# Normalizing after the weighted sum instead of inside the transpose, in the first batch of a fused attention, FFN and MoE kernel

## Chip, cores and metric

One Trainium2 chip, one core. The metric is device time in microseconds for one launch of the whole program (attention for two batches, a SiLU feed-forward layer, a top-1 mixture of eight experts). The median of 3 runs of the kernel before is 621.5 us (619.34 to 621.65). PE is the matmul engine (PEld its weight loads), DVE, ACT and POOL are the three elementwise engines, SP issues most DMAs.

## What is computed

The part of the reference that the change touches is the attention of batch 0 (tiles 0 to 5 of 128 queries; 8 heads of 64):

```python
scores = scale * q @ k.T + bias        # scale = 1/8; local band of 96 keys, 8 global keys
scores = where(keep, scores, -1e9)
scores = scores - max(scores)
a = exp(scores)
a = a / (sum(a) + 1e-09)
x = a @ v                              # then transposed to [heads*64, queries] for the FFN
```

The result x of all 12 tiles (two batches of 6) is what the FFN (x @ w_in, SiLU, @ w_out) reads, and its output goes to the experts.

## The kernel before

The work of the attention is cut into slots: slot s handles tile n = s // 4 and the head pair hp = s % 4. The first batch has SB = 24 slots, written by `slot_b` (L870); the second batch has other code (`slot`, L902) and is not changed. Within the first batch a head pair passes through a software pipeline, and one call of `slot_b(s)` issues a step of several pairs, each engine working its instructions off in the order of issue:

- `emit_qk` (L145): for pair s+1, PE multiplies k and q (64 contraction rows, up to 256 columns) for each of two heads into PSUM tiles `qkp`.
- `emit_tb` (L152): for pair s, DVE adds the bias table and takes the row maximum (L160), one instruction for each head; `emit_mx` (L161) turns the two maxima into the bias of the exponential, -max/8 + ln 1024 (L163).
- `emit_exp` (L164): for pair s-1, ACT computes the exponential of each head and its sum `ss` (L170).
- `emit_dg` (L182): for pair s-1, DVE makes the inverse sums (L185, L186), and POOL multiplies the identity matrix by them, giving a diagonal matrix `dg` for each head (L188).
- `emit_tr` (L189): for pair s-3 (LT = 3), PE multiplies the weights t by `dg` (L194). That transposes and normalizes at once. An f32 product of this kind shows up as two MATMUL instructions. A tile has one chunk of keys (the first tile of the batch) or two (the five others), so a slot has 4 or 8 instructions on L194.
- `emit_cp` (L197): copy from PSUM to SBUF, by ACT from slot 8 on (L199), before that by DVE (L198).
- `emit_px` (L200): for pair s-4, PE multiplies v (64 columns of weights) by the transposed weights (L209), 4 or 8 instructions; the sums of a tile land transposed, ready for the FFN, in a PSUM bank `px` (of tag `pv` for odd tiles, `s1` for even ones).
- `emit_xx` (L212), once a tile: `put_xt` (L243) splits `px` into a high part (ACT, L247) and a low part (DVE, L248), both as fp32r, in the FFN's tile `xT`. For tiles 0 to 3 the low part is put off to the next slot (`xlow`).

The PSUM tiles `qkp` and `tp` come from `abank` (L113), which hands out five banks in turn, three in a slot. From slot 8 on every slot also has one step of decoding the FFN's weights on DVE (`dec_op`, L285; L274 to L276), and at set slots weights are split by ACT and POOL (`spl_w`, L291; L296, L297, L301, L303) and loaded by SP. POOL also copies the eight global keys and values (L139, L142).

After slot 23 the FFN of the first four tiles (chunk 0) begins: each step has 24 products of 128x256 (`s1_mm`, L319; two PSUM banks in turn, tags `s1` and `s1b`), tanh and gating on ACT and DVE, and 12 products of 128x512 (L339 to L341), while DVE decodes and POOL splits the next weights. Slots 24 to 27, which finish the pipeline of the first batch, are worked in between the first two steps.

The lines that hold the order of a slot:

```python
if s+1<SB:
    for j in range(2): emit_qk(*divmod(s+1,4),j)
if o3: cp[0]=emit_tr(n3,h3)
if o1: emit_exp(n1,h1)
...
if cur: emit_tb(n,hp,1); emit_mx(n,hp)
if o3: emit_cp(*cp[0],A if DQ<=s<23 else V)
if o1: emit_dg(n1,h1)
if o4: emit_px(n4,h4)
```

Of the kernel before, what the change touches and what calls it, by code (L numbers as in the profile page):

```python
# [10 lines left out]
F32 = mybir.dt.float32  # L11
# [12 lines left out]
def kernel(ctx, tc, qk, v, n_global, n_local, w_in, w_out, wg, w1, w2, out):  # L24
    nc=tc.nc
    B,NT=v.shape[0],v.shape[1]
    H=8; D=64; KC=4; FB=16; NTT=B*NT; LAG=2; LASTF=2; HB=6; PAIR=256; PX=4
# [3 lines left out]
    SB=24  # L31
    LT=3
# [10 lines left out]
    attn=es_a.enter_context(tc.tile_pool(name="attn",bufs=1,side="right"))  # L43
# [12 lines left out]
    ident=const.tile([P,P],F32,name="ident")  # L56
# [4 lines left out]
    def own_first(n): return n%3==1  # L61
# [10 lines left out]
    V=nc.vector; A=nc.scalar; G=nc.gpsimd; T=nc.tensor; S=nc.sync  # L72
# [62 lines left out]
    def glob_k(n,hp):  # L135

        if n%NT in (0,NT-1): return
        k=ring[hp//2][:,hp%2]
        (G if 4*n<SB else V).tensor_copy(k[:,ksl(n),0,0:32],k[:,ksl(n-1),0,0:32])  # L139
    def glob_v(n):  # L140
        if n%NT in (0,NT-1): return
        if 4*n<SB: G.tensor_copy(vpr4[0:32,n%3,0:512],vpr4[0:32,(n-1)%3,0:512])  # L142
        else: V.tensor_copy(vpr[0:32,n%3],vpr[0:32,(n-1)%3])
    qp={}
    def emit_qk(n,hp,j):  # L145
        i=n%NT
        if (n,hp,j) in qp: return
        q=qp[n,hp,j]=abank([P,2,P],"qkp")
        sl=slice(0,2) if i else slice(0,1)
        w=ring[hp//2][j*D:(j+1)*D,hp%2]; z=ksl(n)  # L150
        T.matmul(q[:,sl],w[:,z,1],w[:,z:z+1,0] if i==0 else w[:,0:3:2,0] if z==0 else w[:,z-1:z+1,0],start=True,stop=True)  # L151
    def emit_tb(n,hp,j):  # L152
        i=n%NT; h=2*hp+j; q=qp.pop((n,hp,j))
        if j==0: tt[n,hp]=attn.tile([P,2,2,P],F32,tag="t",name="t",bufs=3) if 4*n>=SB else mp.tile([P,2,2,P],F32,tag="g",name="t",bufs=6)
        t=tt[n,hp]
        if h==0:
            mx[n]=attn.tile([P,H],F32,tag="mx",name="mx",bufs=2); ss[n]=attn.tile([P,H],F32,tag="ss",name="ss",bufs=2)
        sl=slice(0,2) if i else slice(0,1)
        tb=tabs[:,3:4,h,:] if i==0 else (tabs[:,1::-1,h,:] if i==1 else tabs[:,1:3,h,:]) if own_first(n) else tabs[:,0:2,h,:] if i==1 else tabs[:,2:0:-1,h,:]
        V.tensor_tensor_reduce(out=t[:,j,sl],in0=q[:,sl],in1=tb,scale=1.0,scalar=-3e38,op0=ALU.add,op1=ALU.max,accum_out=mx[n][:,h:h+1])  # L160
    def emit_mx(n,hp):  # L161
        h=2*hp+1
        V.tensor_scalar(out=mx[n][:,h-1:h+1],in0=mx[n][:,h-1:h+1],scalar1=-0.125,scalar2=float(np.log(1024.0)),op0=ALU.mult,op1=ALU.add)  # L163
    def emit_exp(n,hp):  # L164
        i=n%NT
        t=tt[n,hp]
        ce=1 if i==0 else 2
        for j in range(2):
            h=2*hp+j
            A.activation(out=t[:,j,:ce],in_=t[:,j,:ce],func=AF.Exp,scale=0.125,bias=mx[n][:,h:h+1],accum_out=ss[n][:,h:h+1])  # L170
    def emit_h(n,hp):
        t=tt[n,hp]; nch=ce=1 if n%NT==0 else 2
        x=attn.tile([P,2,2,nch,P],F16,tag="hl",name="hl",bufs=2); hl[n,hp]=x
        V.tensor_copy(x[:,:,0],t[:,:,:ce])
    def emit_l(n,hp):
# [2 lines left out]
        y=attn.tile([P,2,2,nch,P],F16,tag="pT",name="pT",bufs=3)  # L178
        pT[n,hp]=y
        S.dma_start_transpose(out=y.rearrange("p a b c d -> p (a b c) d"),in_=x.rearrange("p a b c d -> p (a b c d)"))  # L180
    dg={}
    def emit_dg(n,hp):  # L182

        s=ss[n][:,2*hp:2*hp+2]
        V.tensor_scalar(out=s,in0=s,scalar1=1024.0e-9,scalar2=None,op0=ALU.add)  # L185
        V.reciprocal(out=s,in_=s)  # L186
        d=attn.tile([P,2,P],F32,tag="t",name="dg",bufs=3); dg[n,hp]=d
        for j in range(2): G.tensor_scalar(out=d[:,j],in0=ident,scalar1=s[:,j:j+1],scalar2=None,op0=ALU.mult)  # L188
    def emit_tr(n,hp):  # L189

        t=tt.pop((n,hp)); d=dg.pop((n,hp)); ce=1 if n%NT==0 else 2
        m=abank([P,2,ce,P],"tp")
        for j in range(2):
            for c in range(ce): T.matmul(m[:,j,c],t[:,j,c],d[:,j],start=True,stop=True)  # L194
        y=attn.tile([P,2,ce,P],F32,tag="pT",name="pT4",bufs=3); pT[n,hp]=y
        return y,m
    def emit_cp(y,m,e):  # L197
        if e is V: V.tensor_copy(y,m)  # L198
        else: A.activation(out=y,in_=m,func=AF.Copy)  # L199
    def emit_px(n,hp):  # L200

        i=n%NT; ce=1 if i==0 else 2
        if hp==0: pvt[n]=ps.tile([P,KC,P],F32,tag="pv" if n%2 else "s1",name="px",bufs=1)
        y=pT.pop((n,hp))
        vb=[n%3] if ce==1 else [n%3,(n-1)%3] if own_first(n) else [(n-1)%3,n%3]
        for c in range(ce):
            for j in range(2):
                h=2*hp+j
                T.matmul(pvt[n][j*D:(j+1)*D,hp,:],vpr4[:,vb[c],h*D:(h+1)*D],y[:,j,c,:],start=(c==0),stop=(c==ce-1))  # L209
        if hp==3: glob_v(n)  # L210
    xlow=[]
    def emit_xx(n):  # L212
        put_xt(n,pvt[n],xlow if 4*(n+2)<SB else None)
    def emit_pv(n,hp):
        i=n%NT; ce=1 if i==0 else 2
        if hp==0: pvt[n]=ps.tile([P,H,D],F32,tag="pv",name="pv",bufs=1)
        y=pT.pop((n,hp))
        vb=[n%3] if ce==1 else [n%3,(n-1)%3] if own_first(n) else [(n-1)%3,n%3]
        for j in range(2):
            h=2*hp+j  # L220
            for c in range(ce):
                seq=[(0,0),(0,1),(0,2),(1,0),(1,1)]
                for k,(a,m) in enumerate(seq):
                    T.matmul(pvt[n][:,h,:],y[:,j,a,c,:],vpr[:,vb[c],m,h*D:(h+1)*D],start=(c==0 and k==0),stop=(c==ce-1 and k==4))  # L224
    rs={}
# [11 lines left out]
    def emit_xt(n):  # L237
# [2 lines left out]
        for k in range(KC):  # L240
            T.transpose(m[:,k,:],xa[:,2*k:2*k+2,:].rearrange("p a d -> p (a d)"),ident)
        put_xt(n,m)
    def put_xt(n,m,later=None):  # L243
        c,u=divmod(n,2)
        if u==0: xT[c]=mp.tile([P,2,KC,256],F32R,tag="xT",name="xT",bufs=3)
        sl=xT[c][:,:,:,u*P:(u+1)*P]
        A.activation(out=sl[:,0],in_=m,func=AF.Copy)  # L247
        def low(): V.tensor_tensor(out=sl[:,1],in0=m,in1=sl[:,0],op=ALU.subtract)  # L248
        if later is None: low()
        else: later.append(low)  # L250


    wraw={}; wol={}
# [357 lines left out]
    h1={}; hh={}; yp={}  # L611
# [258 lines left out]
    def slot_b(s):  # L870

        ev=[]
        n,hp=divmod(s,4); n1,h1=divmod(s-1,4); n3,h3=divmod(s-LT,4); n4,h4=divmod(s-LT-1,4)
        cur=s<SB; o1=0<=s-1<SB; o3=0<=s-LT<SB; o4=0<=s-LT-1<SB
        def a_():
            if s<SB-3: want(min(s+WL,SB-1))
            elif cur: want(s+3)
            if s==0:
                for j in range(2): emit_qk(n,hp,j)
            if cur: emit_tb(n,hp,0)  # L880
# [3 lines that stand above are left out]
            if o1: emit_exp(n1,h1)  # L884
        ev.append(a_)
        def a2():
            if cur: emit_tb(n,hp,1); emit_mx(n,hp)
            if o3: emit_cp(*cp[0],A if DQ<=s<23 else V)
            if o1: emit_dg(n1,h1)
            if o4: emit_px(n4,h4)  # L890
            if xlow: xlow.pop()()
        ev.append(a2)
        def b_():
            if cur: glob_k(n,hp)
            if h4==3 and o4: emit_xx(n4)
# [44 lines left out]
    with tc.manual_schedule():  # L940
# [7 lines left out]
        s=0  # L948
# [99 lines left out]
```

## Time and profile before

| | us |
|---|---|
| median of 3 runs | 621.5 |
| the profiled execution's own time | 621.69 |
| its span, first to last instruction | 620.0 |
| PE busy in the span | 590.6 (95%) |
| DVE busy | 389.1 (63%) |
| ACT busy | 303.0 (49%) |
| POOL busy | 186.2 (30%) |
| first batch's slots, from 16.62 to the first FFN product | 55.6 |

Times in rows are us from the start of the span. A matmul's recorded duration contains its way through the array, and the next one starts before it ends; so what a stream of matmuls costs is read from start to start, not from the durations. "PE busy" is for the same reason not a measure of how well PE is used.

### The profile page before, as it was taken

Reading aid. Unit: us, or ns where it says so; the run is one execution under the profiler, and the core shown is the slowest. Engines: PE = TensorE matmul, PEld = TensorE weight load, DVE = VectorE, ACT = ScalarE, POOL = GpSimd, SP = SyncE. Lnnn points to the kernel's source line nnn. Section 1 sums busy time; section 2 is a strip of 40 time slices with the busy share of each in tenths; the row PEclk is TensorE's granted clock in tenths of the full one; section 3 lists DMA queues with packets and bytes.
Section 4 is the critical chain, followed back from the end, with each engine's and each line's share of the span. In section 5 each row is a group of like instructions: output and inputs, shape, how many; then the busy total and the mean of one; then the engine's idle time right before and its main releaser. Section 6 shows DMA issues by size and latency. Waiting matters only on the chain.

```text
span 620.0 us, 12009 instructions
## 1 busy us (share of the span) xinstructions
PE 590.6 (95%) x4054; PEld 500.6 (81%) x4054; DVE 389.1 (63%) x1069; ACT 303.0 (49%) x802; POOL 186.2 (30%) x233
## 2 busy tenths in 40 slices
PE   2999899999999999999999999999899999999996
PEld 1566788888888888888889999888788888888884
DVE  4388669999737764756463345744844678778840
ACT  5377634334353445343532234644653666776641
POOL 3367614444314252131221001112231432331321
PEclk9999999999999999999999999999999999999999
DMA  7639725674355587465444327607845378569500
GB/s 255 243 79 355 218 89 159 215 221 158 116 160 148 149 192 170 106 177 130 115 89 141 86 84 259 254 19 246 263 162 185 127 259 269 184 212 290 162 17 21
DMA packets 81511, 105.18 MB, mean 170 GB/s; under 512 B 29978, under 2 KB 44314, under 8 KB 81441
## 3 DMA queue, kind: packets, MB, share of 16 engines
q1 hardware_dynamic: 75712, 94.79, 50.4%
q0 software_dynamic: 2288, 6.39, 2.8%
q10 hardware_dynamic: 3440, 3.15, 1.6%
q8 instruction: 34, 0.56, 0.4%
q14 instruction: 37, 0.30, 0.2%
HBM read 81.46 MB, written 17.99 MB: 160 GB/s over the span
## 4 chain that ended last, share of the span: by engine, by line
PE 69%; issue 8%; DVE 8%; DMA 6%; ACT 4%; POOL 3%; SPq 1%; ACTq 0%; POOLq 0%; DVEq 0%
PE s L319 17%; PE s L339 6%; PE s L340 5%; PE s L341 5%; PE h L616 5%; PE h L622 4%; PE qkp L151 4%; PE y L639 4%; PE y L641 4%; PE y L640 4%; PE tp L194 3%; PE h L617 2%; POOL wol L303 2%; PE pv L224 2%; PE gl L382 1%
## 5 line engine op out<-in xcount | busy, mean ns | idle before, releaser
L319 PEld LDWEIGHTS s<-xT,wi 128*128 128x128 f32 x1152 | 147.3, 190 | 13.1 <-DVE g L328 6.0
L319 PE MATMUL s<-xT,wi 128*128 128x256 f32 x1152 | 152.2, 284 | 1.9 <-DVE xT L248 1.4
L323 ACT ACTIVATE u<-s 128x256 f32<-128x256 f32 x96 | 35.3, 381 | 112.3 <-PE s L319 111.5
L324 DVE SCALAR_TENSOR_TENSOR s<-u,s 128x256 f32<-128x256 f32 x96 | 39.8, 427 | 79.4 <-ACT u L323 79.4
L339 PE MATMUL s<-woh,g 128*128 128x512 f32 x192 | 79.2, 413 | 0.0
L491 DVE TENSOR_TENSOR uq<-qr,uq 128x512 fp32r<-128x512 f32 x87 | 71.2, 841 | 7.2 <-ACT uq L490 4.4
L340 PE MATMUL s<-woh,g 128*128 128x512 f32 x192 | 75.5, 393 | 0.0
L490 ACT ACTIVATE uq<-qr 128x512 fp32r<-128x512 f32 x112 | 66.4, 626 | 4.4 <-DMA qr<-in_w_dram 4.1
L328 DVE TENSOR_TENSOR g<-s,g 128x256 fp32r<-128x256 f32 x96 | 39.3, 422 | 31.7 <-ACT g L327 27.3
L327 ACT ACTIVATE g<-s 128x256 fp32r<-128x256 f32 x96 | 35.7, 380 | 40.3 <-DVE s L324 40.3
L639 PE MATMUL y<-uq,hh 128*128 128x512 f32 (+6 forms) x136 | 55.2, 406 | 0.0
L641 PE MATMUL y<-uq,hh 128*128 128x512 f32 (+6 forms) x136 | 53.6, 394 | 0.0
L640 PE MATMUL y<-uq,hh 128*128 128x512 f32 (+6 forms) x136 | 53.4, 393 | 0.0
L491 POOL TENSOR_TENSOR uq<-qr,uq 128x512 fp32r<-128x512 f32 x25 | 32.9, 1326 | 62.1 <-ACT uq L490 62.1
L151 PE MATMUL qkp<-ring 64*128 64x256 f32 (+1 forms) x192 | 36.0, 455 | 14.3 <-DMA ring<-in_qk_dram 13.4
L170 ACT ACTIVATE t<-t,mx 128x256 f32<-128x256 f32 (+1 forms) x96 | 45.8, 480 | 6.5 <-DVE mx L163 4.6
L631 ACT ACTIVATE hh<-h 128x224 fp32r<-128x224 f32 (+6 forms) x64 | 23.3, 364 | 47.3 <-DVE h L629 27.3
L632 DVE SCALAR_TENSOR_TENSOR hh<-h,hh 128x224 fp32r<-128x224 f32 (+6 forms) x64 | 25.3, 395 | 31.8 <-ACT hh L631 31.8
L339 PEld LDWEIGHTS s<-woh,g 128*128 128x128 f32 x192 | 36.3, 189 | 7.1 <-ACT u L323 2.0
L340 PEld LDWEIGHTS s<-woh,g 128*128 128x128 f32 x192 | 36.3, 189 | 5.0
L577 POOL DMA_INDIRECT out_dram<-y,ixt x17 | 17.4, 1024 | 74.9 <-ACT y L646 56.7
L341 PE MATMUL s<-wolr,g 128*128 128x512 f32 x128 | 39.6, 390 | 0.0
(215 smaller groups left out, 1071.7 us busy)
## 6 DMA issues: line engine op xcount, KB each, us to landing
qr<-in_w_dram SPq DMA_DIRECT2D x128, 256.0 KB
wolr<-wlo_d SPq DMA_DIRECT2D x64, 256.0 KB
wiraw<-in_w_in_dram SPq DMA_DIRECT2D x16, 512.0 KB
wraw<-in_w_out_dram SPq DMA_DIRECT2D x13, 512.0 KB
xe<-zr SPq DMA_DIRECT2D x8, 792.0 KB
wlo_d<-wol SPq DMA_DIRECT2D x16, 256.0 KB
xw<-xe SPq DMA_DIRECT2D x15, 264.0 KB
ring<-in_qk_dram SPq DMA_DIRECT2D x12, 256.0 KB
```

What stands on the lines that cost most here:

```text
L151: T.matmul(q[:,sl],w[:,z,1],w[:,z:z+1,0] if i==0 else w[:,0:3:2,0] if z==0 else w[:,z-1:z+1,0],start=True,stop=True)
L170: A.activation(out=t[:,j,:ce],in_=t[:,j,:ce],func=AF.Exp,scale=0.125,bias=mx[n][:,h:h+1],accum_out=ss[n][:,h:h+1])
L319: T.matmul(t,w[:,ww,kc,:],x[:,xx,kc,:],start=(k==0),stop=(k==11)); k+=1
L324: V.scalar_tensor_tensor(out=t,in0=u,scalar=1.0,in1=t,op0=ALU.add,op1=ALU.mult)
L339: T.matmul(o,g[u][:,0,sl],wh,start=(f==0),stop=False)
L340: T.matmul(o,g[u][:,1,sl],wh,start=False,stop=False)
L341: else: T.matmul(o,g[u][:,0,sl],wl,start=False,stop=(f==FB-1))
L490: A.activation(out=t[:,0],in_=r,func=AF.Copy)
L491: (G if (i%2 if pool is None else pool) else V).tensor_tensor(out=t[:,1],in0=r,in1=t[:,0],op=ALU.subtract)
L639: T.matmul(o,g[:,0,sl],w[:,0],start=(f==0),stop=False)
L640: T.matmul(o,g[:,1,sl],w[:,0],start=False,stop=False)
L641: T.matmul(o,g[:,0,sl],w[:,1],start=False,stop=(f==7))
```

## The change

The exponentials are transposed as they are, by PE's transpose (one instruction for a 128x128 block instead of two), and the division by the sums moves behind the product with v. For that, once a tile, the inverse sums are made for all 8 heads by two DVE instructions, spread by POOL to 512 columns (`rx`), transposed by four PE transposes (`emit_rb`, a fourth PSUM tile from `abank` in that slot), copied by ACT (`xn`), and multiplied with `px` by DVE. The split into high and low parts moves from ACT and DVE to POOL. Factor -1/8 and maximum are folded: DVE's L160 computes -x/8 and its minimum directly, which removes L163; the factor 1024 goes with it.

```diff
-        V.tensor_tensor_reduce(out=t[:,j,sl],in0=q[:,sl],in1=tb,scale=1.0,scalar=-3e38,op0=ALU.add,op1=ALU.max,accum_out=mx[n][:,h:h+1])
+        if 4*n<SB: V.tensor_tensor_reduce(out=t[:,j,sl],in0=q[:,sl],in1=tb,scale=-0.125,scalar=3e38,op0=ALU.add,op1=ALU.min,accum_out=mx[n][:,h:h+1])
...
-            A.activation(out=t[:,j,:ce],in_=t[:,j,:ce],func=AF.Exp,scale=0.125,bias=mx[n][:,h:h+1],accum_out=ss[n][:,h:h+1])
+            A.activation(out=t[:,j,:ce],in_=t[:,j,:ce],func=AF.Exp,scale=-1.0 if 4*n<SB else 0.125,bias=mx[n][:,h:h+1],accum_out=ss[n][:,h:h+1])
...
-    dg={}
-    def emit_dg(n,hp):
...
-        V.tensor_scalar(out=s,in0=s,scalar1=1024.0e-9,scalar2=None,op0=ALU.add)
-        V.reciprocal(out=s,in_=s)
-        d=attn.tile([P,2,P],F32,tag="t",name="dg",bufs=3); dg[n,hp]=d
-        for j in range(2): G.tensor_scalar(out=d[:,j],in0=ident,scalar1=s[:,j:j+1],scalar2=None,op0=ALU.mult)
...
-            for c in range(ce): T.matmul(m[:,j,c],t[:,j,c],d[:,j],start=True,stop=True)
+            for c in range(ce): T.transpose(m[:,j,c],t[:,j,c],ident)
...
+    def emit_rb(n):
...
+        r=rs.pop(n)
+        m=abank([P,KC,P],"rb")
+        for k in range(KC): T.transpose(m[:,k,:],r[:,k*P:(k+1)*P],ident)
+        x=rb[n]=attn.tile([P,KC,P],F32,tag="t",name="xn",bufs=3)
+        A.activation(out=x,in_=m,func=AF.Copy)
     def emit_xx(n):
-        put_xt(n,pvt[n],xlow if 4*(n+2)<SB else None)
+        x=rb.pop(n)
+        V.tensor_tensor(out=x,in0=pvt[n],in1=x,op=ALU.mult)
+        put_xt(n,x,G)
...
-        A.activation(out=sl[:,0],in_=m,func=AF.Copy)
-        def low(): V.tensor_tensor(out=sl[:,1],in0=m,in1=sl[:,0],op=ALU.subtract)
-        if later is None: low()
-        else: later.append(low)
+        if e: e.tensor_copy(sl[:,0],m)
+        else: A.activation(out=sl[:,0],in_=m,func=AF.Copy)
+        (e or V).tensor_tensor(out=sl[:,1],in0=m,in1=sl[:,0],op=ALU.subtract)
...
-            if cur: emit_tb(n,hp,1); emit_mx(n,hp)
+            if cur: emit_tb(n,hp,1)
             if o3: emit_cp(*cp[0],A if DQ<=s<23 else V)
-            if o1: emit_dg(n1,h1)
+            if o3 and h3==3: emit_rb(n3)
             if o4: emit_px(n4,h4)
-            if xlow: xlow.pop()()
+            if o2 and h2==3:
+                for k in range(2): emit_rs(n2,k)
+                r=attn.tile([P,512],F32,tag="t",name="rx",bufs=3)
+                G.tensor_copy(r.rearrange("p (h d) -> p h d",h=H),rs[n2].to_broadcast([P,H,D])); rs[n2]=r
```

(`e`, where it is given, is POOL; `o2`, `h2` belong to pair s-2.)

## Rows read from the trace of the kernel before

**Rows 1.** Windows by stage: us, each engine's busy us (instructions), PEclk, DMA share, GB/s
```profile
16.62:31.61 14.99, 14.94 (x60) 9.20 (x61) 6.55 (x33) 4.90 (x20) 5.21 (x11) 1.00 0.61 222
31.61:72.26 40.65, 36.80 (x319) 26.78 (x317) 33.56 (x136) 30.63 (x91) 29.62 (x55) 1.00 0.68 219
72.26:83.88 11.62, 11.42 (x105) 10.31 (x105) 5.32 (x13) 3.72 (x12) 3.89 (x21) 1.00 0.70 223
83.88:172.00 88.12, 87.62 (x541) 75.79 (x540) 76.44 (x141) 34.78 (x86) 35.07 (x27) 1.00 0.48 153
```

**Rows 2.** Chain that ended last, at the start: start us, us, what
```profile
8.21 8.28 DMA ring<-in_qk_dram
...
16.62 1.23 PE qkp L151 x4
```

**Rows 3.** Timeline of PE, slots 6, 7 and 10: start us, us, instructions merged
```profile
26.05 1.22 PE L194 MATMUL tp<-dg,t 128*128 128x128 f32 x4
27.20 0.70 PE L209 MATMUL px<-pT,vpr 128*64 128x128 f32 x4
27.82 1.23 PE L151 MATMUL qkp<-ring 64*128 64x256 f32 x4
28.98 2.08 PE L194 MATMUL tp<-dg,t 128*128 128x128 f32 x8
30.98 0.70 PE L209 MATMUL px<-pT,vpr 128*64 128x128 f32 x4
31.61 0.77 PE L151 MATMUL qkp<-ring 64*128 64x256 f32 x4
...
36.82 0.70 PE L151 MATMUL qkp<-ring 64*128 64x256 f32 x4
37.45 1.16 PE L194 MATMUL tp<-dg,t 128*128 128x128 f32 x8
38.54 0.66 PE L209 MATMUL px<-pT,vpr 128*64 128x128 f32 x8
39.13 0.70 PE L151 MATMUL qkp<-ring 64*128 64x256 f32 x4
```

**Rows 4.** Timeline of PE where it transposes later in the kernel
```profile
176.86 0.66 PE L374 MATMUL gt<-ident,xr 128*128 128x128 f32 x4
177.27 0.47 PE L339 MATMUL s<-woh,g 128*128 128x512 f32 x1
...
211.59 0.64 PE L241 MATMUL ms<-ident,xa 128*128 128x128 f32 x4
212.06 0.17 PE L406 MATMUL gr<-geb,upper 128*128 128x8 bf16 x1
```

**Rows 5.** Groups that go, 0 to 140 us: xcount | busy, mean ns | idle before
```profile
L188 POOL TENSOR_SCALAR dg<-ident,ss 128x128 f32<-128x128 f32 x48 | 28.5, 605 | 32.8 <-DVE ss L186 18.4 <-DVE mx L160 8.6 <-ACT g L327 2.3
...
L163 DVE TENSOR_SCALAR mx<-mx 128x2 f32<-128x2 f32 x24 | 5.4, 223 | 0.8
L185 DVE TENSOR_SCALAR ss<-ss 128x2 f32<-128x2 f32 x24 | 4.9, 203 | 5.0 <-ACT t L170 4.8
```

**Rows 6.** Groups near to what is added: the whole span, then POOL's to 140 us
```profile
L234 DVE TENSOR_TENSOR xa<-pv,rs 128x512 f32<-128x512 f32 x6 | 4.0, 675 | 0.0
...
L297 POOL TENSOR_TENSOR wi<-wt,wi 128x512 fp32r<-128x512 f32 x12 | 15.5, 1294 | 23.3 <-ACT wi L296 23.0 <-PE qkp L151 0.2
...
L142 POOL COPY vpr<-vpr 32x512 f32<-32x512 f32 x4 | 2.4, 605 | 0.0
```

**Rows 7.** Windows, sum over twelve slots (36.82 to 66.78 us)
```profile
sum 29.96, PE 27.98 PEld 20.27 DVE 24.44 ACT 22.76 POOL 22.47; mean PE 9.33 PEld 6.76 DVE 8.15 ACT 7.59 POOL 7.49
```

**Rows 8.** Timeline of PE, end of slot 23 and the first FFN product
```profile
70.18 0.66 PE L209 MATMUL px<-pT,vpr 128*64 128x128 f32 x8
72.26 3.13 PE L319 MATMUL s<-xT,wi 128*128 128x256 f32 x24 [1.42 <-DVE xT L248]
75.23 1.05 PE L194 MATMUL tp<-dg,t 128*128 128x128 f32 x8
```

More of the change, by code (lines that the diff above doesn't have):

```diff
@@ L159, in emit_tb @@
         tb=tabs[:,3:4,h,:] if i==0 else (tabs[:,1::-1,h,:] if i==1 else tabs[:,1:3,h,:]) if own_first(n) else tabs[:,0:2,h,:] if i==1 else tabs[:,2:0:-1,h,:]
-        V.tensor_tensor_reduce(out=t[:,j,sl],in0=q[:,sl],in1=tb,scale=1.0,scalar=-3e38,op0=ALU.add,op1=ALU.max,accum_out=mx[n][:,h:h+1])
+        if 4*n<SB: V.tensor_tensor_reduce(out=t[:,j,sl],in0=q[:,sl],in1=tb,scale=-0.125,scalar=3e38,op0=ALU.add,op1=ALU.min,accum_out=mx[n][:,h:h+1])
+        else: V.tensor_tensor_reduce(out=t[:,j,sl],in0=q[:,sl],in1=tb,scale=1.0,scalar=-3e38,op0=ALU.add,op1=ALU.max,accum_out=mx[n][:,h:h+1])
     def emit_mx(n,hp):
@@ L180, in emit_l @@
         S.dma_start_transpose(out=y.rearrange("p a b c d -> p (a b c) d"),in_=x.rearrange("p a b c d -> p (a b c d)"))
-    dg={}
-    def emit_dg(n,hp):
-        s=ss[n][:,2*hp:2*hp+2]
-        V.tensor_scalar(out=s,in0=s,scalar1=1024.0e-9,scalar2=None,op0=ALU.add)
-        V.reciprocal(out=s,in_=s)
-        d=attn.tile([P,2,P],F32,tag="t",name="dg",bufs=3); dg[n,hp]=d
-        for j in range(2): G.tensor_scalar(out=d[:,j],in0=ident,scalar1=s[:,j:j+1],scalar2=None,op0=ALU.mult)
     def emit_tr(n,hp):
-        t=tt.pop((n,hp)); d=dg.pop((n,hp)); ce=1 if n%NT==0 else 2
+        t=tt.pop((n,hp)); ce=1 if n%NT==0 else 2
         m=abank([P,2,ce,P],"tp")
         for j in range(2):
-            for c in range(ce): T.matmul(m[:,j,c],t[:,j,c],d[:,j],start=True,stop=True)
+            for c in range(ce): T.transpose(m[:,j,c],t[:,j,c],ident)
         y=attn.tile([P,2,ce,P],F32,tag="pT",name="pT4",bufs=3); pT[n,hp]=y
@@ L210, in emit_px @@
         if hp==3: glob_v(n)
-    xlow=[]
+    rb={}
+    def emit_rb(n):
[4 more added lines that the diff above has]
+        A.activation(out=x,in_=m,func=AF.Copy)
     def emit_xx(n):
-        put_xt(n,pvt[n],xlow if 4*(n+2)<SB else None)
+        x=rb.pop(n)
+        V.tensor_tensor(out=x,in0=pvt[n],in1=x,op=ALU.mult)
+        put_xt(n,x,G)
     def emit_pv(n,hp):
@@ L228, in emit_rs @@
             rs[n]=attn.tile([P,H,1],F32,tag="rs",name="rs",bufs=2)
-            V.tensor_scalar(out=rs[n][:,:,0],in0=ss[n],scalar1=1024.0e-9,scalar2=None,op0=ALU.add)
+            V.tensor_scalar(out=rs[n][:,:,0],in0=ss[n],scalar1=1e-9 if 4*n<SB else 1024.0e-9,scalar2=None,op0=ALU.add)
         else: V.reciprocal(out=rs[n],in_=rs[n])
@@ L242, in emit_xt, with put_xt @@
         put_xt(n,m)
-    def put_xt(n,m,later=None):
+    def put_xt(n,m,e=None):
         c,u=divmod(n,2)
@@ L873, in slot_b @@
         n,hp=divmod(s,4); n1,h1=divmod(s-1,4); n3,h3=divmod(s-LT,4); n4,h4=divmod(s-LT-1,4)
-        cur=s<SB; o1=0<=s-1<SB; o3=0<=s-LT<SB; o4=0<=s-LT-1<SB
+        n2,h2=divmod(s-2,4); cur=s<SB; o1=0<=s-1<SB; o2=0<=s-2<SB; o3=0<=s-LT<SB; o4=0<=s-LT-1<SB
         def a_():
```

## Prediction

> **What bounds the kernel now.** I read the windows by stage first [rows 1]: from 16.62 us to the first FFN product at 72.26 PE is busy for 51.7 of 55.6 us, no other engine for more than 41, and in the FFN chunk behind it for 87.62 of 88.12 us. So PE sets the pace in both, and a delay of the slots is passed on whole. The chain [rows 2] shows where the slots' clock starts: the load of the second tile's keys and queries ends at 16.48, and PE takes over at 16.62. The change does not touch what lies before.
>
> The main thing is in the timeline of PE [rows 3], read from start to start. In slots 6 and 7 the four scores instructions (L151) take 1.16 us, four of L194 1.15, eight of L194 2.00, four of L209 0.62. In slot 10 the same four scores instructions take 0.63, eight of L194 1.09, eight of L209 0.59. Same forms, same operands in SBUF, almost half the time: before about 31.7 us PE ran at its lower level (1.2 GHz), after it at the upper one (2.4 GHz). The column of the granted clock says 1.00 in both stretches [rows 1], so it doesn't see the lower level here and the durations decide. What did PE do before the rise? In 16.62 to 31.61 it was busy for 14.94 of 14.99 us [rows 1] and stayed low, with slots of four scores, four L194 and four L209 instructions. It rose some 2.7 us after the first batch of eight on L194 began at 28.98, the first tile with two chunks [rows 3]. Being busy was not enough; more full-array products in the slot came just before the rise.
>
> **The transposes.** The change takes away that batch for good: every two-chunk slot gets four transposes where it had eight instructions, a one-chunk slot two where it had four. At the upper level four transposes take 0.41 us (L374) and 0.47 (L241, behind the attention's own products, which is how they will stand here) [rows 4], against 1.09 for eight of L194 [rows 3]. At the lower level no row has them: twice 0.41, so 0.82, is the low bound, and 1.15, four of L194 there [rows 3], the high one. I take twice 0.47, 0.94, since L241 is the nearest row. Eight of L209 at the lower level aren't shown either: 1.08 if they grow from four as L194 does (0.62 x 2.00/1.15), 1.18 if they are twice 0.59; I take 1.10.
>
> So the question is whether the clock still rises at about 31 us. The rows alone speak against it: four instructions in the place of L194 are what the slots had that stayed low. For it speaks only that L209 goes from four to eight. My forecast is that the clock stays low until the FFN's dense products.
>
> The Trainium skill, page "TensorE: Matmul & The Clock Gate", section "Part 4: PE-mode transpose", says the same more sharply: in transpose mode the higher clock doesn't engage, because it doesn't count as PE being busy in the same way. By that rule the time is my forecast's 633 us; were transposes to count as the products do, it could be the first rival's 614. No row before 31.7 us has a transpose, so this trace can't confirm it, and the later transposes [rows 4] run at the upper level amid dense products.
>
> **The sum, with PE at the lower level,** from 16.62 us. Slot 3: 1.16 + 0.47 = 1.63. Slots 4 to 6: 1.16 + 0.47 + 0.62 = 2.25 each, 6.75. Slot 7: 1.16 + 0.94 + 0.62 = 2.72. Slots 8 to 22: 1.16 + 0.94 + 1.10 = 3.20 each, 48.0. Slot 23 has no scores: 2.04. The four transposes of the spread sums (L194's place in slots 6, 10, 14, 18, 22): 5 x 0.94 = 4.7. Together 65.8, so slot 23 ends at 82.5 instead of 70.18 + 0.59 = 70.8 [rows 8]: **+11.7**. With the lower bounds 62.6 (+8.5), with the upper ones 72.2 (+18.0). A slot took 29.96/12 = 2.50 before [rows 7]; it gains up to slot 7 (28.7 against 31.6) and loses 0.7 in every later one.
>
> *First FFN product.* It waits for the PSUM bank `s1`, that is for tile 4's `px` to be read by ACT and then DVE: 72.26 - 70.8 = 1.5 us [rows 8]. After the change one DVE product frees it; L234, of that shape, takes 0.675 [rows 6], so with its release 0.75: **-0.7**. Next in line would be nothing, since tiles 0 to 3 were split four slots earlier.
>
> *The rise then.* The FFN's products start at the lower level. It rose 2.7 us after the first batch of eight; I take 2.7 to 5.4 us of dense work at half speed, so 1.3 to 2.7 lost, **+2.0**. *Slots 24 to 26* between the FFN's first steps, PE busy for 11.42 of 11.62 us [rows 1]: three batches at 0.47 in place of 1.09 and one more spread, at the upper level, **-1.4**.
>
> +11.7 - 0.7 + 2.0 - 1.4 = +11.6. Against the profiled execution's own 621.69 us that is 633.3; the median of the runs shown, 621.5, is 0.2 less. I forecast **633 us**; its own range by the bounds is 629 to 640.
>
> **What I cost at nothing, and under what cover.** DVE loses L163 (24 x 0.223) and L185 and L186 (24 x about 0.2 each), some 14 us in all [rows 5]; its two new small ones and the product replace, once a tile, L248. POOL loses 48 x 0.605 = 28.5 us on L188 [rows 5] and gets, six times, a spread copy and a high-part copy (0.605 for 512 columns of 32 partitions, L142, as low bound; 1.294, L297, as high) and the low part (1.294) [rows 6]: 15 to 23 us. Neither was the pace-setter: DVE has 24.44/12 = 2.04 us of work in a slot and POOL 1.9 [rows 7]. ACT keeps its load, since the copy of the transposed sums replaces L247: 1.90 a slot. All this hides in slots of 3.2 us. Without the cover (upper level) ACT's 1.90 is next to bind.
>
> On POOL's queue the split of a tile (1.9 to 2.6 us) now waits for DVE's product, and behind it stand the copy of the global keys for the next slot, needed some slots on, the weights' low parts (L303, whose stores on SP have weight loads queued behind them) and the global values (L142), which L209 reads a tile later. A tile has four slots, 12.8 us; POOL's work in them is under 9. No DMA is added or moved; the loads that ACT issues in slots 4 to 7 come earlier by at most 3 us. A fourth PSUM tile in a slot makes the next slot's transposes take the bank of the scores that DVE reads last in that very slot. DVE's 1.4 us are done within 3.2; without that, at most 1.4 - 0.63 = 0.8, five times, 4 us, which the upper bound of the range partly takes in.
>
> **Rivals.** *Faster: the clock rises all the same,* because L209's eight and the transposes suffice. Place: PE, slots 8 to 14. Then a slot has 0.63 + 0.47 + 0.59 = 1.69 us on PE, 1.90 on ACT, 1.4 on DVE; with the spread and imperfect overlap I take 2.1, a gain of 0.4. Rising at slot 11: -2.9 to slot 7, 3 x 0.7 + 0.9 = +3.0 for slots 8 to 10, 13 x -0.4 = -5.2, then -0.7 and -1.4: -7.2, **614 us**. At slot 8 it would be 610, at slot 14 619; at slot 17 it decides nothing. For it: the change of 4 to 8 on L209, and that the slots are packed more tightly. Against it: the fifteen low microseconds of a busy PE [rows 1].
>
> *No change:* the rise comes between slots 14 and 20, gain and loss cancel: 619 to 625, so **622 us**. The same comes out if the FFN chunk takes up the delay, which its 87.62 busy of 88.12 us [rows 1] speak against.
>
> *The change doesn't do what it says:* if a 128x128 f32 transpose cost as much as its two instructions, L194 would stay at 2.00 and 1.09, and the clock with it; then only the spreads count, one at 2.00 and five at 1.09, less the 0.7: +6.8, **628 us**. The 0.41 and 0.47 for four [rows 4] all but exclude it.
>
> **How the numbers follow.** A measurement of this kernel can tell about 0.5% (3.1 us) from no change. Low clock through the slots: 0.65, slower by 8 to 18 us. Rise early: 0.25, nearly all of it faster by over 3 us. Rise late or delay absorbed: 0.10, within 0.5%; the transposes that gain nothing are within the 0.65. So faster 0.25, same 0.10, slower 0.65. The predicted time is the likeliest case's, 633. Its own range is 629 to 640; most of the chance lies on both sides of zero, so the range of 8 in 10 runs from 614, which takes in the slower half of the early rises and the late ones, to 639.
>
> **What would show it.** In the profile after: four scores instructions still 1.16 us from start to start at 40 and 60 us; slots 3.2 us apart; ACT and DVE under 6 of 10 us busy there; the first FFN product at 82 to 84 us, and its 24 products falling from some 5 to 3 us within two steps; then everything shifted, nothing stretched. Wrong would be: scores at 0.63 us before 45 us; slots at 2.1 us with ACT full; or a first FFN product before 73 us. If the clock is low but slots take over 3.5 us, a wait of the transposes on DVE or POOL is the error of the sum.

## Result and profile after

The changed kernel takes 611.16 us (median, 609.94 to 611.58), the kernel before, run beside it, 620.87. The ratio is 0.9842, interval 0.982 to 0.9864: 1.6% faster, where I had forecast 633 us and slower. It is below the range too. In the comparisons further below, with more runs, the kernel before has a median of 619.3 and the changed one, run again, of 611.04. The profiled execution took 611.58 us, its span 609.9 against 620.0.

The windows by stage of the changed kernel, the second cut at its own first FFN product, the third in the FFN behind it (us, busy us and instructions of PE, PEld, DVE, ACT, POOL, then PEclk, DMA share, GB/s):

```profile
16.62:31.61 14.99, 14.27 (x75) 7.52 (x76) 8.45 (x35) 7.74 (x30) 3.39 (x8) 1.00 0.67 240
31.61:63.92 32.31, 28.09 (x248) 17.91 (x246) 23.72 (x84) 27.08 (x81) 17.99 (x30) 1.00 0.77 265
75.00:172.00 97.00, 96.59 (x601) 84.10 (x601) 79.25 (x153) 39.75 (x100) 36.97 (x29) 1.00 0.51 163
```

Against [rows 1]: the slots end 8.3 us sooner, PE now stands idle for 4.2 of the 32.3 us of their second part (before, 3.9 of 40.7), and the FFN behind is as dense as it was. The start is nearly the same (16.38 against 16.62). So the gain is made in the slots and handed on.

The timeline of PE of the changed kernel, slots 6 to 9, then some of the places where it waits (start us, us, instructions merged; in brackets the idle time before and what ended it):

```profile
22.95 1.23 PE L151 MATMUL qkp<-ring 64*128 64x256 f32 x4
24.11 0.69 PE L187 MATMUL tp<-ident,t 128*128 128x128 f32 x2
24.59 1.06 PE L209 MATMUL rb<-ident,rx 128*128 128x128 f32 x4
25.58 0.70 PE L202 MATMUL px<-pT,vpr 128*64 128x128 f32 x4
26.21 1.00 PE L151 MATMUL qkp<-ring 64*128 64x256 f32 x4
27.14 0.66 PE L187 MATMUL tp<-ident,t 128*128 128x128 f32 x4
27.73 0.44 PE L202 MATMUL px<-pT,vpr 128*64 128x128 f32 x4
28.09 0.70 PE L151 MATMUL qkp<-ring 64*128 64x256 f32 x4
29.52 0.66 PE L187 MATMUL tp<-ident,t 128*128 128x128 f32 x4 [0.72 <-DVE mx L160]
30.10 0.66 PE L202 MATMUL px<-pT,vpr 128*64 128x128 f32 x8
30.69 0.70 PE L151 MATMUL qkp<-ring 64*128 64x256 f32 x4
...
48.68 0.70 PE L151 MATMUL qkp<-ring 64*128 64x256 f32 x4 [0.80 <-DMA ring<-in_qk_dram]
...
59.32 0.70 PE L151 MATMUL qkp<-ring 64*128 64x256 f32 x4
...
63.92 3.14 PE L320 MATMUL s<-xT,wi 128*128 128x256 f32 x24 [0.86 <-DVE xn L214]
```

The four scores instructions take 1.16 us from start to start at 22.95 and 0.63 at 28.09: PE reached its upper level in slot 7's scores, at about 26.8 us, some 5 us sooner than before [rows 3] and before any two-chunk tile was transposed. From there a slot takes (59.32 - 28.09)/14 = 2.23 us, against (66.78 - 31.61)/14 = 2.51. Four transposes cost 0.59 start to start (27.14 to 27.73) where eight of L194 cost 1.09.

What PE waits for in 16 to 75 us, changed kernel (us in total, times, longest), then two lines of the same view of the kernel before:

```profile
PE qkp L151 <- DMA ring<-in_qk_dram: 3.0, 3, 1.7
PE tp L187 <- DVE mx L160: 2.5, 4, 0.7
PE s L320 <- DVE xn L214: 0.9, 1, 0.9
PE rb L209 <- DVE mx L160: 0.3, 1, 0.3
```

```profile
PE qkp L151 <- DMA ring<-in_qk_dram: 1.8, 1, 1.8
PE tp L194 <- DVE mx L160: 1.2, 3, 0.8
```

One wait has grown and one is new. The transposes waited for DVE before as well, 1.2 us in three; now the first transposes of four tiles wait 2.5. New is that the scores of slots 17 and 21 wait for the load of keys and queries (0.80 and 0.47; the 1.7 is the one at the start).

### The profile page after: what moved, and what is told of

Read it like the earlier page. It is cut to its first block, busy times and chain, and to the rows that moved or that the text cites. A ratio compares the mean times of both kernels' runs of the same rounds, so it can differ in the third digit from the quotient of the medians.

```text
span 609.9 us, 11756 instructions
## 1 busy us (share of the span) xinstructions
PE 580.1 (95%) x3990; PEld 489.3 (80%) x3990; DVE 377.1 (62%) x1009; ACT 302.9 (50%) x802; POOL 172.6 (28%) x203
## 4 chain that ended last, share of the span: by engine, by line
PE 67%; DMA 9%; issue 9%; DVE 7%; ACT 3%; POOL 3%; SPq 0%; POOLq 0%; DVEq 0%; ACTq 0%
PE s L320 18%; PE s L340 6%; PE s L341 6%; PE s L342 6%; PE h L623 4%; DMA ring<-in_qk_dram 4%; PE h L617 4%; PE qkp L151 4%; PE y L640 3%; PE y L642 3%; PE y L641 3%; PE h L618 2%; PE pv L226 2%; POOL wol L304 2%; DMA out_dram<-y,ixt 2%
## 5 line engine op out<-in xcount | busy, mean ns | idle before, releaser
L320 PEld LDWEIGHTS s<-xT,wi 128*128 128x128 f32 x1152 | 147.5, 190 | 12.0 <-DVE g L329 5.6
L320 PE MATMUL s<-xT,wi 128*128 128x256 f32 x1152 | 152.0, 284 | 1.4 <-DVE xn L214 0.9
L151 PE MATMUL qkp<-ring 64*128 64x256 f32 (+1 forms) x192 | 35.7, 452 | 14.5 <-DMA ring<-in_qk_dram 14.5
L633 DVE SCALAR_TENSOR_TENSOR hh<-h,hh 128x224 fp32r<-128x224 f32 (+6 forms) x64 | 25.3, 395 | 31.8 <-ACT hh L632 31.8
L578 POOL DMA_INDIRECT out_dram<-y,ixt x17 | 17.4, 1024 | 75.7 <-ACT y L647 55.8
```

Source lines behind the costliest of these rows:

```text
L320: T.matmul(t,w[:,ww,kc,:],x[:,xx,kc,:],start=(k==0),stop=(k==11)); k+=1
```

## Experiments

Three things had to be told apart: what raises the clock, whether the transposes or the rise carry the gain, and what limits the slots now. The kernel before has a median of about 619.3 us in all the comparisons below. "First FFN product" is the start of the first batch on L319 (L320 after the change), a place beyond all that the change touches but its last three slots; before 72.26, changed 63.92. A rise is read from the scores on L151 going from 1.16 to 0.63 us from start to start; the tenths are from the trace's clock records, the first of which begins there. Each rise and each first FFN product is that of one execution.

| kernel | rise, about us | first FFN product | median us | ratio to before |
|---|---|---|---|---|
| before, run again | 30 | 72.27 | 619.34 | 0.9997 [0.997, 1.0023] |
| changed, run again | 26 | 63.92 | 611.04 | 0.9868 [0.9826, 0.991] |
| extra transposes, slots 3 to 5 | 20.7 | 62.94 | 609.36, one run | |
| extra products, slots 3 to 5 | 21.3 | 63.43 | 609.32, one run | |
| transposes as plain products | 25.6 | 71.24 | 619.73 | 1.0003 [0.9981, 1.0024] |
| changed, early products | 15 | 60.37 | 607.31 | 0.9812 [0.977, 0.9853] |
| before, early products | 15 | 66.53 | 615.5 | 0.9942 [0.9924, 0.996] |
| fold and split undone | 28.7 | 71.51 | 619.54 | 0.9995 [0.9963, 1.0027] |
| split alone undone | 28.8 | 71.56 | 618.93 | 0.9993 [0.9973, 1.0014] |
| split undone, low part put off | 27 | 65.36 | 613.97 | 0.9923 [0.9902, 0.9943] |
| fold alone undone | 26 | 65.08 | 612.77 | 0.9888 [0.985, 0.9927] |

### Does a transpose raise the clock?

Four more transposes of the identity in slots 3 to 5, or two more products of it (four instructions), into a PSUM bank that is free then:

```diff
+            if 3<=s<6:
+                w=ps.tile([P,KC,P],F32,tag="s1b",name="extra",bufs=1)
+                for k in range(4): T.transpose(w[:,k],ident,ident)
```

> The changed kernel with four more transposes (identity by identity, into a PSUM bank not used then, result not read) in each of slots 3, 4 and 5. T1: the clock rises before slot 6's spread, at 20 to 24 us. T2 (transposes don't count): no sooner than 26.9 us, later by the two to three us that the additions cost at the lower level. Total within 2 us of the changed kernel either way.

```diff
+                for k in range(2): T.matmul(w[:,k],ident,ident,start=True,stop=True)
```

> As the run with four more transposes, but with two f32 products (four matmul instructions, identity by identity) in each of slots 3, 4 and 5. T1: the rise comes at the same time as with the four transposes, within one us or so. T2: it comes at 20 to 24 us here and at 26.9 or later there.

One run each, without an interval: 609.36 and 609.32 us. The timeline of PE with the extra transposes, then with the extra products:

```profile
19.41 1.23 PE L151 MATMUL qkp<-ring 64*128 64x256 f32 x4
20.57 0.48 PE L187 MATMUL tp<-ident,t 128*128 128x128 f32 x2
20.88 0.60 PE L892 MATMUL extra<-ident 128*128 128x128 f32 x4
21.41 0.44 PE L202 MATMUL px<-pT,vpr 128*64 128x128 f32 x4
21.78 0.70 PE L151 MATMUL qkp<-ring 64*128 64x256 f32 x4
```

```profile
19.37 1.23 PE L151 MATMUL qkp<-ring 64*128 64x256 f32 x4
20.52 0.69 PE L187 MATMUL tp<-ident,t 128*128 128x128 f32 x2
21.00 0.77 PE L892 MATMUL extra<-ident 128*128 128x128 f32 x4
21.70 0.44 PE L202 MATMUL px<-pT,vpr 128*64 128x128 f32 x4
22.07 0.70 PE L151 MATMUL qkp<-ring 64*128 64x256 f32 x4
```

The clock rises in slot 4 in both, at 20.7 and 21.3 us, 5 to 6 us sooner than in the changed kernel. It rose as early behind extra transposes as behind extra products, in one execution of each; in the one with transposes only slot 3's four stood ahead of the rise, those of slot 4 began at 20.88.

Then I took the four spread transposes out (`rb`), the one dense batch that the change puts into slot 6. This kernel leaves the division by the sums out; for its outputs the program then takes its general path, 3,578 us in all, so only the first 65 us are read.

```diff
-        x=rb.pop(n)
-        V.tensor_tensor(out=x,in0=pvt[n],in1=x,op=ALU.mult)
+        x=attn.tile([P,KC,P],F32,tag="t",name="xn",bufs=3)
+        V.tensor_scalar(out=x,in0=pvt[n],scalar1=1.0,scalar2=None,op0=ALU.mult)
...
-            if o3 and h3==3: emit_rb(n3)
...
-            if o2 and h2==3:
-                for k in range(2): emit_rs(n2,k)
...
```

> The changed kernel without the spread sums of the first batch (no inverse sums, no spread copy, no four transposes a tile; DVE's product becomes a copy of the same shape), so the first batch is not divided by its sums. Theory T1 (transposes count for PE's clock as products do; it rose at 26.9 us because slot 6 has six transposes in a row): without them the rise comes later, with tile 1's four transposes a slot, between 28 and 34 us. Theory T2 (transposes don't count; the rise came from the scores and L202 alone): the rise comes at 26.9 us or sooner. Theory T3 (it is the spread's batch alone that raised it, four transposes a slot would not): low level until the first FFN product, slots of 3.2 us, about 10 us slower than before. By T1 the spread costs five times 0.5 us of PE and the waits on its PSUM bank, five times 0.6 us: the first FFN product 4 to 5 us sooner than in the changed kernel if the rise were as early, 2 to 4 with the later rise; total 607 to 610 us.

Its timeline of PE, slots 5 to 7:

```profile
20.97 1.23 PE L151 MATMUL qkp<-ring 64*128 64x256 f32 x4
22.13 0.69 PE L187 MATMUL tp<-ident,t 128*128 128x128 f32 x2
22.74 0.70 PE L202 MATMUL px<-pT,vpr 128*64 128x128 f32 x4
23.37 1.23 PE L151 MATMUL qkp<-ring 64*128 64x256 f32 x4
24.53 0.46 PE L187 MATMUL tp<-ident,t 128*128 128x128 f32 x2
24.92 0.44 PE L202 MATMUL px<-pT,vpr 128*64 128x128 f32 x4
25.29 0.70 PE L151 MATMUL qkp<-ring 64*128 64x256 f32 x4
```

The clock rose at about 24.6 us in a row of slots with just four scores, two transposes and four products: less in each than in those slots of the kernel before that I took to be too thin. So the rise came without the dense batch. The first FFN product came at 61.99, 1.9 us sooner than in the changed kernel, with the two later waits for loads grown to 1.53 each.

Of the theories set out above, T1 missed here: it had the rise at 28 to 34 us. By itself this run fits T2, by which transposes don't count; T2 missed in the run with extra transposes, where it had 26.9 or later and 20.7 was measured. How far chance goes is shown by the changed kernel's PE instructions up to slot 7, which were traced in eight executions (the changed kernel twice and six variants below): they rose at 26.0 to 28.8 us. This thinner stream rose at 24.6, and 20.7 and 21.3 lie 3 us and more ahead of all nine. So the two runs with extra work stand out, but whether a transpose counts as a product does is not shown by one execution of each.

### Is it the transposes, or the earlier rise?

The changed kernel with L187 as plain products, two instructions for a block again, the spread and the split as changed:

```diff
-            for c in range(ce): T.transpose(m[:,j,c],t[:,j,c],ident)
+            for c in range(ce): T.matmul(m[:,j,c],t[:,j,c],ident,start=True,stop=True)
```

> The changed kernel with the transposes undone: plain f32 products by the identity, two instructions for a block, everything else of the change kept. If the gain is PE's shorter slot (theory P): a slot has 0.63 + 1.09 + 0.59 = 2.31 us of PE again, plus the spread, and the first FFN product comes at 69 to 72 us, total 617 to 621 us. If the gain came from the work taken off DVE and POOL and the shorter waits (theory Q): the slots stay at 2.2 to 2.35 us, total 611 to 614 us. The clock rises at 26.9 us or sooner, since slot 6 has eight such instructions in a row.

Its timeline of PE, the scores of slots 6, 8 and 22:

```profile
24.85 1.07 PE L151 MATMUL qkp<-ring 64*128 64x256 f32 x4
...
29.50 0.70 PE L151 MATMUL qkp<-ring 64*128 64x256 f32 x4
...
65.89 0.70 PE L151 MATMUL qkp<-ring 64*128 64x256 f32 x4
```

619.73 us, ratio 1.0003: the whole gain is gone, though the clock rose at 25.6, sooner than in the changed kernel. Slots took (65.89 - 29.50)/14 = 2.60 us. So without the halved transposes there is nothing to gain, and the rise was no gift of theirs alone: through slot 5 this kernel has the PE instructions of the kernel before, which rose at 31.8. To see how firm such a moment is, both kernels were run once more as they are:

> The kernel before, once more, unchanged. Theory F (the prediction's reading: the clock rises when the first eight instructions of L194 come): the rise is again at 31 to 32 us, behind slot 7's transposes. Theory S (the moment of the rise is not set by the mix of a slot; it scatters from execution to execution, and 31.8 us was a late one): it comes somewhere between 20 and 32 us, more than 1 us away from 31.8, and the first FFN product comes sooner by up to half of the difference.

> The changed kernel, once more, unchanged. Theory F: the rise is again at 26 to 27.5 us, in slot 6 with its six transposes. Theory S: it comes somewhere between 20 and 32 us, and not at the same place in the order of instructions. Its time is 609 to 612 us either way.

Before: rise at 30.1 instead of 31.8, now inside slot 7's eight and the first time in slot 8's scores, and the first FFN product at 72.27 against 72.26. The scores of slot 8 came 0.64 us sooner (30.97 against 31.61), but later waits took that back, the longest at slot 17:

```profile
54.91 0.70 PE L151 MATMUL qkp<-ring 64*128 64x256 f32 x4 [1.24 <-DVE dct L274]
```

Changed: 26.2 instead of 26.9. Next the clock was brought up before the slots, by products of the identity while PE waits for the first loads, in the changed kernel and, the same lines, in the kernel before:

```diff
             if cur: emit_tb(n,hp,0)
+            if s in (2,3):
+                w=ps.tile([P,KC,P],F32,tag="s1b",name="extra",bufs=1)
+                for k in range(8 if s==2 else 4): T.matmul(w[:,k%KC],ident,ident,start=True,stop=True)
```

> The changed kernel with twelve f32 products more (identity by identity, result not read) while PE waits for the first loads, eight ahead of slot 2's scores and four ahead of slot 3's. If the low level up to 27 us costs time: the clock rises before 18 us, slots 3 to 6 take about 1.9 us instead of 2.4 and the first FFN product comes 3 to 5 us sooner, total 606 to 608 us. If the loads set the pace of these slots: the clock rises as early, but scores wait for loads and at most 1.5 us are gained, 609.5 to 611 us.

> The kernel before with the twelve products of early work. The clock rises at about 15 us. If the low level was worth as much there as in the changed kernel or more (it lasted 3 to 5 us longer): the first FFN product comes 4 to 6 us sooner, 614 to 616 us, and the change is then worth 8 to 9 us with the clock up as well. If a part of the change's gain was an earlier rise: more than 6 us sooner, 612 to 614 us, and the change is worth 5 to 7.

The timeline of PE of the changed kernel with early products:

```profile
16.76 0.70 PE L151 MATMUL qkp<-ring 64*128 64x256 f32 x4 [0.69 <-DMA ring<-in_qk_dram]
17.39 0.44 PE L187 MATMUL tp<-ident,t 128*128 128x128 f32 x2
...
60.37 3.14 PE L320 MATMUL s<-xT,wi 128*128 128x256 f32 x24 [0.86 <-DVE xn L214]
```

The scores take 0.63 us from the second tile on. It gives 3.7 us on the changed kernel (611.04 to 607.31) and 3.9 on the one before (619.36 to 615.5). The change itself is worth 615.5 - 607.31 = 8.2 us with the clock up in both and 619.3 - 611.0 = 8.3 without: by the medians the rise and the gain are apart. The traces say so less clearly: at the first FFN product the two kernels are 66.53 - 60.37 = 6.2 us apart with early products and 8.3 without, but both profiled executions of the kernel before (621.69 and 621.8 us) lie above its median. The changed kernel with early products is the fastest of all that were run.

### What limits the slots now?

I first suspected the fourth PSUM tile of a slot and gave the spread's transposes a bank of their own:

```diff
-        m=abank([P,KC,P],"rb")
+        m=ps.tile([P,KC,P],F32,tag="s1" if n%2 else "pv",name="rb",bufs=1) if n<5 else abank([P,KC,P],"rb")
```

> The changed kernel with the spread sums of tiles 0 to 4 in the PSUM bank that the other tile's product with v has left free, so that the five banks of the scores and transposes keep their turn. If the transposes' waits on DVE (2.5 us in four, and 0.3 for the spread itself) come from that fourth bank: they go, and the slots end up to 2.8 us sooner, 608.5 us; since the scores then wait more for their loads, as in the run without the spread, 1 us or more of it comes back: 609 to 610 us. If the waits come from elsewhere: nothing changes.

611.52 us, 0.9891 [0.9844, 0.9937]. The wait of `rb` (0.3) went; the four waits of `tp` for DVE stayed (0.81, 0.60, 0.60, 0.57 us), so they are not the bank's. Then DVE's product with the inverse sums of tiles 0 to 3 was put behind the next slot's maxima, alone, and together with the bank and the early products:

```diff
+    xlate=[]
...
             if o4: emit_px(n4,h4)
+            if xlate: emit_xx(xlate.pop())
...
-            if h4==3 and o4: emit_xx(n4)
+            if h4==3 and o4:
+                if n4<4: xlate.append(n4)
+                else: emit_xx(n4)
```

> The changed kernel with DVE's product of tiles 0 to 3 put off into the next slot, behind that slot's two score instructions on DVE. The waits of the transposes on L160 (2.5 us in four) stand in the first slot of each tile. If they come from DVE's product, which waits for the last product with v and stands ahead of the next tile's scores on DVE's queue: they go, 1.5 to 2.5 us gained at the first FFN product, 608.5 to 610 us. If they come from the fourth PSUM bank (the run with the other bank speaks against it): nothing changes, 611 us.

> The changed kernel with three of the edits together: the product put off by a slot, the spread in the other tile's PSUM bank, and the twelve products of early work. If they add up: 3.5 us of the early work and 2 of the other two, 605 to 606 us. If the loads of keys and queries set the pace then: their waits grow to 3 us and more and the time stays at 606.5 to 607.5 us.

What PE waits for in 16 to 75 us with the product put off, and a stretch of its windows (columns as above):

```profile
PE qkp L151 <- DMA ring<-in_qk_dram: 4.2, 2, 2.5
...
PE tp L187 <- DVE mx L160: 0.3, 1, 0.3
```

```profile
49.90:53.20 3.30, 3.30 (x19) 1.99 (x17) 1.60 (x8) 2.09 (x6) 1.41 (x2) 0.50 1.10 388
```

The transposes' waits fell from 2.5 to 0.3 us: DVE's product, queued ahead of the next tile's maxima, was their cause. Nothing was gained: 612.79 us alone (0.9907 [0.9875, 0.9938]) and 608.01 with all (0.9827 [0.9803, 0.9852]), no better than the early products alone. What PE no longer waits for DVE it waits for the loads, now 2.5 us at once ahead of slot 17's scores (48.95 us), and after that the granted clock fell to 0.50 for a while. In the changed kernel the loads already move 316 GB/s with the 16 engines busy for 0.91 of 36 to 62 us (283 and 0.86 in the 26 us up to 66 before). In the window shown they moved 388 GB/s, as much as in the same stretch of the kernel before (385). So a shorter slot meets the loads, as far as these rows tell; no run with fewer or earlier loads was made.

### What do the other parts bring?

Fold (L160, the scale, the factor 1024, L163 again) and split were put back as before, the transposes and the spread kept; of the diff two places:

```diff
-        put_xt(n,x,G)
+        put_xt(n,x)
...
-            if cur: emit_tb(n,hp,1)
+            if cur: emit_tb(n,hp,1); emit_mx(n,hp)
```

> The changed kernel with its other parts undone: maximum, scale and factor 1024 as before (DVE's L163 is back, 24 small instructions), and the split into high and low parts back on ACT and DVE. The transposes, the spread and DVE's product stay. If these parts gain nothing beside PE's slots: 610.5 to 612 us. If the freed DVE and ACT time counts now that PE's slot is short (ACT's 1.9 us a slot next to bind): 612.5 to 615 us.

A miss: 619.54 us (613.51 to 622.55), 0.9995, the whole gain gone though PE's instructions are those of the changed kernel. I had both parts down at nothing. So each was undone by itself, and the split once more with its low part put off by a slot, as the kernel before does (`xlow`):

> The changed kernel with the split of x back on ACT (high part) and DVE (low part, right behind it), the rest as changed. Theory Q (queue: the low part waits for ACT on DVE's queue, ahead of the next tile's maxima): the first transposes of tiles after 30 us wait about 2 us for DVE, as where both parts were undone; first FFN product 69 to 72 us; 617 to 620 us, ratio 0.995 to 1.001. Theory F (the fold carries it, DVE being short of time): waits under 1 us, first FFN product 64 to 66 us, 611 to 613 us, ratio 0.985 to 0.990.

> The changed kernel with the maximum and the scale as before (24 DVE steps of 0.223 us more), the rest as changed. Theory Q: DVE has the 0.2 us of a slot free, the waits of each tile's first transposes stay at 0.6 to 0.9 us, first FFN product 63.5 to 65.5 us, 610.5 to 612.5 us, ratio 0.985 to 0.990. Theory F: first FFN product 68 to 72 us, 616 to 620 us, ratio 0.993 to 1.001.

> The split back on ACT and DVE, but the low part of tiles 0 to 3 put off to the next slot, as in the kernel before. Theory Q: DVE no longer waits for ACT ahead of the next tile's maxima; the waits of each tile's first transposes fall to 0.6 to 1.2 us; what is left of the loss is ACT's and DVE's extra work, 611 to 615 us, ratio 0.986 to 0.993. If it is not the order but DVE's and ACT's load that costs: waits stay near 2 us, 617 to 620 us.

The split alone: 618.93 us, 0.9993. The fold alone: 612.77, 0.9888, an interval that overlaps both of the changed kernel's. The split with the low part put off: 613.97, 0.9923. What PE waits for with the split back on ACT and DVE (L250 and L251 there), the timeline of DVE at the end of a tile, of PE at slot 8's scores and the first FFN product, and windows:

```profile
PE tp L187 <- DVE mx L160: 8.1, 4, 2.1
PE qkp L151 <- DMA ring<-in_qk_dram: 1.8, 1, 1.8
```

```profile
40.81 0.69 DVE L214 TENSOR_TENSOR xn<-px,xn 128x512 f32<-128x512 f32 x1 [2.16 <-ACT pT L192]
42.19 0.69 DVE L251 TENSOR_TENSOR xT<-xn,xT 128x512 fp32r<-128x512 f32 x1 [0.69 <-ACT xT L250]
42.80 0.42 DVE L160 CUSTOM_DVE_ANT_1 t<-qkp,tabs 128x256 f32<-128x256 f32 x1
```

```profile
29.22 0.70 PE L151 MATMUL qkp<-ring 64*128 64x256 f32 x4
...
71.56 3.13 PE L320 MATMUL s<-xT,wi 128*128 128x256 f32 x24 [0.86 <-DVE xn L214]
```

```profile
28.80:32.10 3.30, 1.19 (x10) 0.57 (x10) 2.44 (x6) 1.82 (x6) 0.00 (x0) 1.00 0.09 30
32.20:35.50 3.30, 3.30 (x18) 2.00 (x18) 2.50 (x11) 1.67 (x7) 0.84 (x3) 0.50 0.14 48
...
62.90:66.30 3.40, 3.40 (x19) 2.09 (x18) 2.65 (x13) 2.09 (x6) 1.34 (x2) 0.50 0.61 199
```

DVE makes its product, stands 0.69 us until ACT has made the high part, makes the low part, and only then takes the next tile's maxima, for which exponential and transposes wait. Each tile's first transposes then wait 2.0 to 2.1 us instead of 0.6 to 0.7: 8.1 - 2.5 = 5.6 us more. After two of the four waits the granted clock fell to 0.50 for some 3.3 us; from these transposes to the second next scores 4.50 and 4.51 us pass where the changed kernel takes 2.98 (29.52 to 32.50), so 3.0 us more for both. The loads' waits of 0.80 and 0.47 us and the spread's of 0.26 are gone, 1.5 us. Slot 8's scores stand 1.1 us later (29.22 against 28.09): the slots started 0.46 later, and the rise came at 28.8. 5.6 + 3.0 - 1.5 + 1.1 = 8.2; measured 71.56 - 63.92 = 7.6. The 0.6 between them are stops of PE in the changed kernel that are too short for the view of waits.

With the low part put off the waits are back at 0.6 to 0.7 and most of the gain with them, so it is mostly the order of DVE's queue that costs. The 2.9 us that are still missing (613.97 against 611.04) were not followed up; that trace has one wait of PE that the changed kernel lacks, 1.23 us at slot 17 for DVE's decoding (L278).

## Why the prediction was wrong

**The step that failed is "my forecast is that the clock stays low until the FFN's dense products".** I had seen one rise, found the first eight of L194 just ahead of it, and took the one for the cause. The runs put three facts in its place: the clock rose at 26.9 and 26.2 us in the changed kernel, and even at 24.6 in slots with two transposes each; with the same PE instructions as before it rose some five us sooner (25.6 against 30.1 and 31.8); and it rose sooner yet in the two runs with extra work, transposes or products (20.7, 21.3). By the page "TensorE: Matmul & The Clock Gate" of the Trainium skill, "Part 4: PE-mode transpose", the higher clock does not engage in transpose mode. Here four f32 transposes took 0.99 us at the lower level and 0.59 at the upper, and the clock rose ahead of the FFN in every trace of the kernel that makes them, so the measurement decides against that rule for this kernel, and against the 633 us that I had drawn from it. Whether a transpose counts towards the rise as a product does stays open: the run with extra transposes speaks for it, the one without the spread does not, one execution each. I had noted that this trace could not confirm the rule, and should have let that weigh more. Slots 8 to 22 at the lower level, the +14.6 that turned -2.9 into the sum's +11.7, never came. The rivals of no change and of transposes that cost two instructions fell with the same rows.

**The first rival's case came, but not for its reason.** The clock rose all the same, yet in slot 7, before the first eight of the product with v (30.10 us) that the rival leans on, and before slots 8 to 14, where it has its place. For a rise at slot 11 it told 614 us, for one at slot 8 610; measured are 611. Its terms:
- Up to slot 8's scores: -2.9 by the sum, -3.5 measured (28.09 against 31.61), 0.24 of it an earlier start. The low slots were dearer than told (3: 1.77 for 1.63; 4 and 5: 2.40 for 2.25, as two transposes with L202 behind them take 0.62 and not 0.47), but the rise in slot 7 won more.
- Low slots 8 to 10, +3.0 in the rival: none. That is the missing 3 us; the errors of the other terms nearly cancel.
- A slot at the upper level: 2.1 told, 2.23 measured, so 14 x (2.23 - 2.51) = -3.9. My 2.1 had room for overlap; the 1.81 of a slot without a wait (30.69 to 32.50) is close to the 1.69 told for PE.
- From there to the first FFN product -0.9, of which its wait is 1.42 to 0.86, -0.56 (told -0.7).
- Slots 24 to 26: -1.4 told; the lead grows from 8.34 at the first FFN product to 9.78 at 119 us, -1.4. But only 0.8 of it comes in these slots (third batch of FFN products at 83.88 against 74.74, a lead of 9.14); 0.6 is gained in the FFN's next three steps, up to 102 us, where the two kernels have the same PE instructions. Why is open, and that the term fits is luck.
- Sum: -3.5 - 3.9 - 0.9 - 1.4 = -9.8 before rounding, of the span's -10.1; the rest comes after 430 us. These are two profiled executions; by the medians of the later comparisons the change is worth 8.3.

**The prices of the transposes nearly held:** four at the lower level 0.99 (24.59 to 25.58; told 0.94), at the upper 0.59 with L202 behind (told 0.47; with the spread's four behind they take 0.49, in the changed kernel with extra transposes from 32.13 to 32.62).

**What I costed at nothing.** The fold: right, at most 1.2 us of the first FFN product, not told apart in the medians. The split on POOL: right only as the change has it. I looked at what stands behind it on POOL's queue and not at what its going saves on DVE's, where in this order it is worth the whole gain (618.93 us without it). The cover "ACT's 1.90 is next to bind" was wrong: with slots at 2.23 the waits of PE are for DVE's order and the loads, none for ACT directly, which is busy for 27.08 of 32.31 us. Of the signs that I had named for being wrong, scores at 0.63 before 45 us and a first FFN product before 73 us came, a full ACT did not. The fourth bank: bounded at 4 us, measured 0.3.

**Not settled:** what sets the moment of the rise, and why the clock of the kernel before rises at 30 to 32 us and that of its near copy (the transposes as plain products) at 25.6. The two have other data in the same products (a spread diagonal against the identity, weights with the factor 1024); one changed alone was not tried. Chance is the rival: eight executions with the PE instructions of the changed kernel up to slot 7 had the rise at 26.0 to 28.8 us, a spread of 2.8, and the near copy was traced once. Between the two traces of the kernel before, 1.7 us of it were worth nothing at the first FFN product.

## What to carry to other kernels

One rise of the clock in a trace tells when it came, not what brought it: run the kernel more than once and put dense work elsewhere before building a forecast on its cause. Halving PE's work in a pipelined slot pays only as far as the other queues let it; look for the long instruction once a tile that stands ahead of what PE waits for, above all one that itself waits for another engine. If PE waits for its first loads, a few products in that wait are worth what the lower level costs (here 3.8 us, with or without the change).

## What was not expected of the hardware

- The moment of the rise is loose: 31.8 and 30.1 us in two executions of one kernel, 26.9 and 26.2 in two of the other, 28.7 and 28.8 in two of its variants with the same PE instructions up to there; 9 to 15 us behind the start of the slots.
- A wait of PE of 2.0 to 2.5 us in the midst of the slots was followed by a granted clock of 0.50 in some cases and not in others: two of four waits of 2.0 to 2.1 us with the split undone, one of four with fold and split undone, the one of 2.5 us with the product put off, and not one of 2.1 us with all three edits together. The column of the granted clock shows those falls, while it says 1.00 in the first 26 us at the lower level.
- A 128x128 f32 transpose is one instruction and about half a product's time at either level: 0.99 against 2.00 us at the lower, 0.59 against 1.09 at the upper, four blocks each.
